# Taking three bits of each weight on ScalarE instead of with a VectorE shift, and a softplus whose sign step reads SBUF

## The chip, the cores and the metric

The kernel runs on one core of a Trainium2 chip. The metric is device time in microseconds. The kernel before takes 617.2 us in the median of 3 runs (616.24 to 618.05).

## What is computed

Inputs are float32 for the attention and float64 for the weights of the two layers. A decaying linear attention (retention) over 2 batches, 8 heads, 768 positions and 64 dimensions gives 1536 tokens of 512 numbers, which then pass two MLP layers of 512 to 2048 to 512. In the reference, cut to what matters:

```python
for t in range(S):
    state = gamma * state + einsum('bhd,bhe->bhde', k[:, :, t], v[:, :, t])
    y[:, :, t] = scale * einsum('bhd,bhde->bhe', q[:, :, t], state)
x = y.transpose(0, 2, 1, 3).reshape(B * S, H * D)

h = x @ w_in                                             # first layer
g = maximum(h, 0) + log1p(exp(-abs(h)))
x = (g @ w_out).astype(float32)

h = x @ w2_in                                            # second layer
x = (h * clip(h + 3, 0, 6) / 6 @ w2_out).astype(float32)
```

## The kernel before

**Products.** Every large product is made of 3 fp32r matmuls: each operand is held as a hi part and a lo part, and hi by hi, hi by lo and lo by hi are summed in PSUM. The names tell the parts: `x_hi` and `x_lo` are the layer's input, `hi` and `lo` the parts of g, `w_parts` holds both parts of a weight chunk.

**Stages.** The attention goes by 12 units of 128 rows. The first four stand in program order. From there on (`nc.on = False`, L310) a planner chooses the order on each engine, and units 4 to 11 are interleaved with the first 8 steps of the first layer (L148 to L154). A layer has 3 chunks of 512 tokens with 16 steps each. A step (L408) does `gemm1` for one block of 128 of the 2048 hidden numbers, 12 matmuls of 128x512 into a PSUM bank h, then the activation to g, hi and lo (L351 to L366), and `gemm2` for the block of two steps earlier (LAG = 2), 12 more matmuls into four held accumulators. A bank comes from eight, four of which are held by the accumulators while the others rotate (L130).

**Weights.** They are float64 in memory, and the 64 chunks of 128 by 512 (32 a layer) are made into two fp32r parts on the chip. `fetch` (L73) loads 512 KB of raw words on SP's queue into one of three `raw` buffers. `convert` (L83) takes the high word y and the low word of each number. ScalarE scales y as a float in place (L89), VectorE clamps it (L90), shifts it by 3 into w (L91), sets the sign bit (L92), and ors in the low word shifted right by 29 (L93). The first 8 chunks then have a ScalarE copy to the hi part and a GpSimd subtraction for the lo part (L96, L97). The other 56 have a negated ScalarE copy to the lo part, a DMA from GpSimd's queue that adds w to it in place (the accumulate transfer, L100), and the ScalarE copy to the hi part. The buffer w has few copies in its pool, so the first operation that writes w waits for the accumulate transfer of an earlier chunk to land.

**When.** `feed` (L119) is called in the steps of the first layer's first chunk (its own weights), in its third chunk (the second layer's w_in, one a step, L415), and in the second layer's first chunk (w_out, L417). Each engine runs its instructions in order, so one that waits holds those behind it. In the trace nearly all instructions carry L31, the line of the helper that records them; tiles are read by name: `raw<-raw` is L89 on ACT and L90 on DVE, `w<-raw` L91, `w<-raw,w` L92 and L93, `w_parts<-w` L96, L99 and L101 on ACT and the accumulate transfer on POOL, `g<-banks` and `e<-g,banks` are L355 and L356, `e<-e` L357, `g<-g,e` L358, `pt` and `qT,kT` the scores of the attention.

Of the kernel before, what the change touches and what calls it, by code (L numbers as in the profile page):

```python
# [10 lines left out]
F32 = mybir.dt.float32  # L11
F32R = mybir.dt.float32r
U32 = mybir.dt.uint32
AF = mybir.ActivationFunctionType
ALU = mybir.AluOpType
PSUM = bass.MemoryType.PSUM
P = 128
# [23 lines left out]
@with_exitstack  # L41
def kernel(ctx, tc, q, k, v, w1_in, w1_out, w2_in, w2_out, tq, tk, tc_, tg, out):
    nc = InOrder(tc)
    B, H, S, D = q.shape
    NT, DM = out.shape
    DFF = w1_in.shape[1]
    NP = H // 2
    KD = DM // P
    NF = DFF // P
    C = P  # L50
    NCH = S // C
    CH = 512
    chunks1 = [(0, 0, 512), (1, 0, 512), (2, 0, 512)]
    chunks2 = [(0, 0, 512), (1, 0, 512), (2, 0, 512)]
    LAG = 2
    EARLY = 4

    tc.nc.scalar.preload_act_table_set("softplus")

    xpool = ctx.enter_context(tc.tile_pool(name="xpool", bufs=1))  # L60
    x_hi = [xpool.tile([P, KD, CH], F32R, name=f"x_hi{c}") for c in range(NT // CH)]
    x_lo = [xpool.tile([P, KD, CH], F32R, name=f"x_lo{c}") for c in range(NT // CH)]

    win_p = ctx.enter_context(tc.tile_pool(name="win", bufs=NF))
    wout_p = ctx.enter_context(tc.tile_pool(name="wout", bufs=NF))
    psum = ctx.enter_context(tc.tile_pool(name="psum", bufs=1, space=PSUM))
    raw_p = ctx.enter_context(tc.tile_pool(name="raw", bufs=3))
    cv_p = ctx.enter_context(tc.tile_pool(name="cv", bufs=2))

    w_in_t, w_out_t, raws = {}, {}, {}  # L70
    words = {0: (w1_in.bitcast(U32), w1_out.bitcast(U32)), 1: (w2_in.bitcast(U32), w2_out.bitcast(U32))}

    def fetch(m, o, f):  # L73
        raw = raw_p.tile([P, CH, 2], U32, tag="raw", name="raw")
        src = words[m][o]
        if o:
            nc.sync.dma_start(out=raw.rearrange("p n t -> p (n t)"), in_=src[f * P:(f + 1) * P, :])
        else:
            nc.sync.dma_start(out=raw.rearrange("p (k n) t -> p k (n t)", k=KD),
                              in_=src[:, 2 * f * P:2 * (f + 1) * P].rearrange("(k p) f -> p k f", p=P))  # L80
        raws[m, o, f] = raw

    def convert(m, o, f):  # L83

        raw = raws.pop((m, o, f))
        low, y = raw[:, :, 0], raw[:, :, 1]

        w = cv_p.tile([P, CH], U32, tag="w", name="w")
        nc.scalar.activation(y.bitcast(F32), y.bitcast(F32), AF.Copy, scale=2.0 ** -112)  # L89
        nc.vector.tensor_scalar(y.bitcast(F32), y.bitcast(F32), -TOP, TOP, ALU.max, ALU.min)  # L90
        nc.vector.tensor_scalar(w, y, 3, None, ALU.logical_shift_left)  # L91
        nc.vector.scalar_tensor_tensor(w, y, 0x80000000, w, ALU.bitwise_and, ALU.bitwise_or)  # L92
        nc.vector.scalar_tensor_tensor(w, low, 29, w, ALU.logical_shift_right, ALU.bitwise_or)  # L93
        t = (wout_p if o else win_p).tile([P, 2, CH], F32R, tag="w", name="w_parts")
        if done[1] < 2 * EARLY:
            nc.scalar.activation(t[:, 0], w.bitcast(F32), AF.Copy)  # L96
            nc.gpsimd.tensor_tensor(t[:, 1], w.bitcast(F32), t[:, 0].bitcast(F32), ALU.subtract)  # L97
        else:
            nc.scalar.activation(t[:, 1], w.bitcast(F32), AF.Copy, scale=-1.0)  # L99
            nc.gpsimd.dma_start(out=t[:, 1].bitcast(F32), in_=w.bitcast(F32), accum_op=ALU.add)  # L100
            nc.scalar.activation(t[:, 0], w.bitcast(F32), AF.Copy)  # L101
        if o:
            w_out_t[m, f] = t
        else:
            w_in_t[m, f] = t.rearrange("p a (k n) -> p a k n", k=KD)

    NU = B * NCH
    order = [(0, 0, f) for f in range(EARLY)]
    for f in range(NF):
        order += [(0, 1, f)] + [(0, 0, f + EARLY)] * (f + EARLY < NF)  # L110
    order += [(1, 0, f) for f in range(NF)] + [(1, 1, f) for f in range(NF)]
    done = [0, 0]

    def fetch_weights(n):
        while done[0] < min(len(order), n):
            fetch(*order[done[0]])
            done[0] += 1

    def feed(n):  # L119

        n = min(n, len(order))
        while done[1] < n:
            fetch_weights(done[1] + (1 if nc.on else 2))
            convert(*order[done[1]])
            done[1] += 1

    banks = psum.tile([P, 8, CH], F32, name="banks")
    free = list(range(8))

    def bank(hold=False):  # L130

        i = free.pop(0)
        if not hold:
            free.append(i)
            return banks[:, i, :]
        return i, banks[:, i, :]

    def release(i):
        free.append(i)

    def first(f):
        return EARLY + 2 * (f + 1) - max(0, f + 1 + EARLY - NF)

    step, last, n_steps = moe(ctx, tc, nc, out, x_hi, x_lo, w_in_t, w_out_t, chunks1, chunks2, NF, KD, DM, CH, LAG, feed, first, bank, release)
    s = 0
    with ExitStack() as actx:
        unit = attention(actx, tc, nc, q, k, v, tq, tk, tc_, tg, x_hi, x_lo, CH, bank, feed, fetch_weights)
        for u in range(CH // P, NU):  # L148
            begin, end = unit(u)
            begin()  # L150
            step(s, True, False)
            end()
            step(s, False, True)
            s += 1  # L154
    while s < n_steps:
        step(s)
        s += 1
# [175 lines left out]
def moe(ctx, tc, nc, out, x_hi, x_lo, w_in_t, w_out_t, chunks1, chunks2, NF, KD, DM, CH, LAG, feed, first, bank, release):  # L333
# [7 lines left out]
    def gemm1(m, c, ci, f):  # L341
        xi, o, n = c
        w = w_in_t[m, f]
        h = bank()[:, :n]
        i = 0
        for kk in range(KD):
            xh, xl = x_hi[xi][:, kk, o:o + n], x_lo[xi][:, kk, o:o + n]
            for a, bb in ((w[:, 0, kk, :], xh), (w[:, 0, kk, :], xl), (w[:, 1, kk, :], xh)):
                nc.tensor.matmul(h, a, bb, start=(i == 0), stop=(i == 3 * KD - 1))
                i += 1  # L350
        e = wk.tile([P, CH], F32, tag="e", name="e")[:, :n]  # L351
        g = wk.tile([P, CH], F32, tag="g", name="g")[:, :n]
        if m == 0:

            nc.scalar.activation(g, h, AF.Relu)  # L355
            nc.vector.scalar_tensor_tensor(e, g, -2.0, h, ALU.mult, ALU.add)  # L356
            nc.scalar.activation(e, e, AF.Softplus)  # L357
            nc.vector.tensor_tensor(g, g, e, ALU.add)  # L358
        else:
            nc.scalar.activation(e, h, AF.Relu, bias=cw)  # L360
            nc.vector.scalar_tensor_tensor(g, e, 6.0, h, ALU.min, ALU.mult)
        hi = gp.tile([P, CH], F32R, tag="hi", name="hi")[:, :n]
        lo = gp.tile([P, CH], F32R, tag="lo", name="lo")[:, :n]
        nc.scalar.activation(hi, g, AF.Copy)
        nc.vector.tensor_tensor(lo, g, hi.bitcast(F32), ALU.subtract)
        g_t[m, ci, f] = hi, lo  # L366
# [41 lines left out]
    def step(s, one=True, two=True):  # L408
        if one and s < len(steps):
            m, c, ci, f = steps[s]  # L410
            gemm1(m, c, ci, f)
            if m == 0 and ci == 0:
                feed(first(f))
            if m == 0 and ci == n1 - 1:
                feed(2 * NF + f + 1)  # L415
            if m == 1 and ci == 0:
                feed(3 * NF + f + 1)  # L417
        if two and LAG <= s < len(steps):
            gemm2(*steps[s - LAG])
        if two and s == len(steps):  # L420
            gemm2(*steps[s - LAG], *(f for _, _, _, f in steps[s - LAG + 1:]))
# [40 lines left out]
```

## Time and profile before

| What | Before |
|---|---|
| runs | 616.24, 617.2, 618.05 us, median 617.2 |
| profiled execution | span 613.8 us; its own time is not given apart |
| TensorE (PE) busy | 598.1 us, 97% of the span |
| VectorE (DVE) busy | 351.8 us, 57% |
| ScalarE (ACT) busy | 275.9 us, 45% |
| GpSimd (POOL) busy | 103.4 us, 17% |
| DMA | 61.60 MB moved, mean 100 GB/s |

The span runs from the first to the last instruction of one execution, and the time of a run has 3.4 us more in the median. Busy shares are means over stretches that differ. In 40 slices of 15.3 us, DVE is at 9 tenths or more from the fourth slice to the tenth, and at 2 or 3 tenths from the 27th on, while PE is at 9 from the fifth slice on, but for the last.

### The profile page before, as it was taken

What the parts mean: (1) busy time and instruction counts of PE and PEld (TensorE: products, weight loads), DVE (VectorE), ACT (ScalarE), POOL (GpSimd) and SP (SyncE); (2) the same over time, 40 slices, a digit from 0 to 9 for tenths busy, and PEclk for the clock granted to TensorE, in tenths of its full rate; (3) what the DMA queues carried; (4) which work ended last, traced back from release to release, by engine and by line L of the source; (5) the groups of instructions that cost most, each with busy time, mean ns of one, the idle gap of its engine ahead of it and who ended that gap; (6) DMA issues with size and microseconds to landing.
All of it is one profiled execution on the core that took longest, in us unless ns stands there. A gap on an engine that the chain in (4) does not pass through costs nothing.

```text
span 613.8 us, 7743 instructions
## 1 busy us (share of the span) xinstructions
PE 598.1 (97%) x2963; PEld 491.2 (80%) x2963; DVE 351.8 (57%) x583; ACT 275.9 (45%) x473; POOL 103.4 (17%) x110
## 2 busy tenths in 40 slices
PE   7988999999999999999999999999999999999997
PEld 6865778788788888888887878888888888888886
DVE  4589999999773334376667798832322222322223
ACT  3355475678563333465556687722222222222220
POOL 1745664432100000011111122200000000000000
PEclk9998999999999999999999999999999999999999
DMA  9998888799600000045566689600100000100001
GB/s 193 236 229 211 219 197 208 192 217 227 159 32 0 1 0 1 9 111 119 140 180 154 162 208 262 125 7 1 68 1 0 1 1 0 70 1 1 0 1 69
DMA packets 69510, 61.60 MB, mean 100 GB/s; under 512 B 40032, under 2 KB 56672, under 8 KB 69472
## 3 DMA queue, kind: packets, MB, share of 16 engines
q1 hardware_dynamic: 61408, 46.42, 26.6%
q0 software_dynamic: 8064, 14.68, 14.6%
q8 instruction: 23, 0.38, 0.3%
q14 instruction: 15, 0.12, 0.1%
HBM read 43.26 MB, written 3.15 MB: 76 GB/s over the span
## 4 chain that ended last, share of the span: by engine, by line
PE 66%; DVE 13%; issue 7%; DMA 6%; ACT 3%; POOL 2%; SPq 1%; DVEq 0%; POOLq 0%; ACTq 0%
PE banks L31 66%; DVE w L31 6%; DMA raw<-in_moe_w_in_dram 3%; DVE raw L31 2%; POOL w_parts L31 2%; DMA w_parts<-w 2%; DVE g L31 1%; SPq L31 1%; DVE pt L31 1%; DMA q<-in_q_dram 1%; DVE lo L31 1%; ACT e L31 1%; DVE e L31 1%; ACT raw L31 1%; ACT w_parts L31 1%
## 5 line engine op out<-in xcount | busy, mean ns | idle before, releaser
L31 PE MATMUL banks<-x_hi,w_parts 128*128 128x512 f32 x768 | 253.9, 391 | 2.4 <-POOL w_parts L31 1.2
L31 PEld LDWEIGHTS banks<-x_hi,w_parts 128*128 128x128 f32 x768 | 143.8, 188 | 34.4 <-POOL w_parts L31 2.1
L31 PE MATMUL banks<-x_lo,w_parts 128*128 128x512 f32 x384 | 149.6, 390 | 0.0
L31 PE MATMUL banks<-hi,w_parts 128*128 128x512 f32 x384 | 129.4, 397 | 0.9 <-POOL w_parts L31 0.8
L31 PE MATMUL banks<-w_parts,hi 128*128 128x512 f32 (+1 forms) x386 | 118.4, 388 | 0.7 <-DVE g L31 0.7
L31 DVE SCALAR_TENSOR_TENSOR g<-e,banks 128x512 f32<-128x512 f32 x48 | 33.0, 687 | 123.3 <-ACT e L31 123.3
L31 DVE SCALAR_TENSOR_TENSOR w<-raw,w 128x512 uint32<-128x512 uint32 x128 | 94.3, 738 | 1.6
L31 DVE TENSOR_TENSOR lo<-g,hi 128x512 fp32r<-128x512 f32 x96 | 66.3, 690 | 48.9 <-ACT hi L31 48.6
L31 POOL DMA_DIRECT2D w_parts<-w x56 | 49.3, 880 | 251.9 <-DVE e L31 98.7
L31 ACT ACTIVATE hi<-g 128x512 fp32r<-128x512 f32 x96 | 60.5, 630 | 65.0 <-DVE g L31 61.6
L31 ACT ACTIVATE e<-banks,three 128x512 f32<-128x512 f32 x48 | 32.9, 686 | 125.7 <-PE banks L31 125.7
L31 ACT ACTIVATE w_parts<-w 128x512 fp32r<-128x512 f32 x120 | 70.4, 625 | 39.2 <-DVE w L31 39.0
L31 PEld LDWEIGHTS banks<-hi,w_parts 128*128 128x128 f32 x384 | 72.8, 190 | 17.6 <-POOL w_parts L31 1.5
L31 PEld LDWEIGHTS banks<-w_parts,hi 128*128 128x128 f32 x386 | 72.3, 188 | 16.0 <-DVE g L31 1.1
L31 PEld LDWEIGHTS banks<-x_lo,w_parts 128*128 128x128 f32 x384 | 72.1, 188 | 14.9
L31 PE MATMUL banks<-lo,w_parts 128*128 128x512 f32 x192 | 75.6, 394 | 0.4 <-DVE lo L31 0.4
L31 PE MATMUL banks<-w_parts,lo 128*128 128x512 f32 (+1 forms) x193 | 74.9, 388 | 0.0
L31 DVE SCALAR_TENSOR_TENSOR e<-g,banks 128x512 f32<-128x512 f32 x48 | 32.7, 682 | 27.5 <-ACT g L31 27.5
L31 DVE TENSOR_TENSOR g<-g,e 128x512 f32<-128x512 f32 x48 | 34.4, 717 | 23.9 <-ACT e L31 23.5
L31 ACT ACTIVATE raw<-raw 128x512 f32<-128x512 f32 x64 | 42.2, 669 | 12.7 <-DMA raw<-in_moe_w_in_dram 12.7
L31 ACT ACTIVATE g<-banks 128x512 f32<-128x512 f32 x48 | 28.2, 587 | 36.5 <-PE banks L31 36.5
L31 PEld LDWEIGHTS banks<-lo,w_parts 128*128 128x128 f32 x192 | 36.5, 190 | 8.9 <-DVE lo L31 1.5
(45 smaller groups left out, 401.1 us busy)
## 6 DMA issues: line engine op xcount, KB each, us to landing
raw<-in_moe_w_in_dram SPq DMA_DIRECT2D x32, 512.0 KB, 4.2
raw<-in_moe_w_out_dram SPq DMA_DIRECT2D x32, 512.0 KB, 4.6
w_parts<-w POOLq DMA_DIRECT2D x56, 256.0 KB, 4.9
q<-in_q_dram SPq DMA_DIRECT2D x12, 256.0 KB, 5.3
v<-in_v_dram SPq DMA_DIRECT2D x12, 256.0 KB, 4.9
k<-in_k_dram SPq DMA_DIRECT2D x11, 256.0 KB, 5.3
out_dram<-ob SPq DMA_DIRECT2D x11, 256.0 KB, 2.0
k<-in_k_dram SPq DMA_DIRECT2D x2, 128.0 KB, 2.8
```

The lines of the kernel that those rows point to most:

```text
L31: ins = getattr(self.engine, op)(*args, **kwargs)
```

## The change

Both parts leave the results of the layer what they were.

The conversion no longer shifts y on VectorE into w. A new ScalarE operation reads the low word as an integer, scales it by a little under 2 to the -29, adds a constant a little under -0.5 from a tile `half` of one number per partition, takes Relu, and writes w as an unsigned integer from 0 to 7. The first VectorE merge sets the sign bit on it as before, and the second now shifts y by 3 and ors w to it. So VectorE has three operations a chunk instead of four, ScalarE has one more, and the first to write w is on ScalarE.

In the softplus, ScalarE copies h instead of taking Relu of it. VectorE sets the sign bit of the copy in SBUF, which gives -|h| (before: -2 Relu(h) + h, which read h in PSUM). The last VectorE step is max(g, 0) + e with two sources, as before g + e. Nothing but the ScalarE copy reads the PSUM bank.

```diff
+    half = raw_p.tile([P, 1], F32, tag="half", name="half", bufs=1)
+    nc.vector.memset(half, -0.5 + 7.5 * 2.0 ** -12)
...
         nc.scalar.activation(y.bitcast(F32), y.bitcast(F32), AF.Copy, scale=2.0 ** -112)
+        nc.scalar.activation(w, low, AF.Relu, scale=2.0 ** -29 * (1 - 2.0 ** -12), bias=half)
         nc.vector.tensor_scalar(y.bitcast(F32), y.bitcast(F32), -TOP, TOP, ALU.max, ALU.min)
-        nc.vector.tensor_scalar(w, y, 3, None, ALU.logical_shift_left)
         nc.vector.scalar_tensor_tensor(w, y, 0x80000000, w, ALU.bitwise_and, ALU.bitwise_or)
-        nc.vector.scalar_tensor_tensor(w, low, 29, w, ALU.logical_shift_right, ALU.bitwise_or)
+        nc.vector.scalar_tensor_tensor(w, y, 3, w, ALU.logical_shift_left, ALU.bitwise_or)
...
-            nc.scalar.activation(g, h, AF.Relu)
-            nc.vector.scalar_tensor_tensor(e, g, -2.0, h, ALU.mult, ALU.add)
+            nc.scalar.activation(g, h, AF.Copy)
+            nc.vector.tensor_scalar(e.bitcast(U32), g.bitcast(U32), 0x80000000, None, ALU.bitwise_or)
             nc.scalar.activation(e, e, AF.Softplus)
-            nc.vector.tensor_tensor(g, g, e, ALU.add)
+            nc.vector.scalar_tensor_tensor(g, g, 0.0, e, ALU.max, ALU.add)
```

The planner then orders the engines anew. Three places show what moves.

ScalarE at the first steps of the first layer's third chunk, where the second layer's weights begin to be converted (`w_parts` are the two copies of a chunk, DMASW stands for the accumulate transfer). Before:

```order
L31 ACTIVATE raw<-raw 128x512 [waits DMAHW6_49]
L31 ACTIVATE g<-banks 128x512 [waits PE_49,Activation_49]
L31 ACTIVATE w_parts<-w 128x512 x2
L31 ACTIVATE e<-e 128x512 [waits DVE_49]
L31 ACTIVATE hi<-g 128x512 [waits DVE_49,PE_49]
L31 ACTIVATE g<-banks 128x512 [waits PE_49,Activation_49]
L31 ACTIVATE w_parts<-w 128x512 [waits DVE_49]
L31 ACTIVATE w_parts<-w 128x512
L31 ACTIVATE e<-e 128x512 [waits DVE_49]
L31 ACTIVATE raw<-raw 128x512 [waits DMAHW7_49]
```

Now:

```order
L31 ACTIVATE raw<-raw 128x512 [waits DMAHW6_49]
L31 ACTIVATE g<-banks 128x512 [waits PE_49]
L31 ACTIVATE w_parts<-w 128x512 x2
L31 ACTIVATE e<-e 128x512 [waits DVE_49]
L31 ACTIVATE hi<-g 128x512 [waits DVE_49,PE_49]
L31 ACTIVATE w<-raw,half 128x512 [waits DMASW2_49,Activation_49]
L31 ACTIVATE g<-banks 128x512 [waits PE_49]
L31 ACTIVATE w_parts<-w 128x512 x2
L31 ACTIVATE e<-e 128x512 [waits DVE_49]
L31 ACTIVATE raw<-raw 128x512 [waits DMAHW7_49]
L31 ACTIVATE hi<-g 128x512 [waits DVE_49,PE_49]
L31 ACTIVATE w<-raw,half 128x512 [waits DMASW3_49,Activation_49]
```

The new operation stands ahead of the scaling of `raw` and of the copy of h, and it carries a wait for an accumulate transfer, which in the rows before no ScalarE instruction has.

VectorE at the same place, before:

```order
L31 TENSOR_SCALAR w<-raw 128x512 [waits DMASW3_49]
L31 SCALAR_TENSOR_TENSOR w<-raw,w 128x512 [waits DVE_49]
L31 TENSOR_SCALAR raw<-raw 128x512 [waits DMAHW0_49,Activation_49]
L31 SCALAR_TENSOR_TENSOR w<-raw,w 128x512 [waits DVE_49]
L31 SCALAR_TENSOR_TENSOR e<-g,banks 128x512 [waits Activation_49]
L31 TENSOR_TENSOR g<-g,e 128x512 [waits Activation_49]
L31 TENSOR_TENSOR lo<-g,hi 128x512 [waits Activation_49]
L31 TENSOR_SCALAR w<-raw 128x512 [waits DMASW4_49]
```

Now:

```order
L31 SCALAR_TENSOR_TENSOR w<-raw,w 128x512 [waits DMASW3_49,Activation_49]
L31 TENSOR_SCALAR raw<-raw 128x512 [waits DMAHW0_49,Activation_49]
L31 SCALAR_TENSOR_TENSOR w<-raw,w 128x512 [waits DVE_49]
L31 TENSOR_SCALAR e<-g 128x512 [waits Activation_49]
L31 SCALAR_TENSOR_TENSOR g<-g,e 128x512 [waits Activation_49]
L31 TENSOR_TENSOR lo<-g,hi 128x512 [waits Activation_49]
L31 SCALAR_TENSOR_TENSOR w<-raw,w 128x512 [waits DMASW4_49,Activation_49]
```

The shift with its wait for the transfer is gone, and the first merge waits for ScalarE too.

TensorE in an attention unit beside the first chunk (`qT,kT` are the scores). Before:

```order
L31 MATMUL banks<-hi,w_parts 128x512
L31 MATMUL banks<-qT,kT 128x128 [waits DVE_49]
L31 MATMUL banks<-qT,kT 128x128 x3
L31 MATMUL banks<-hi,w_parts 128x512
L31 MATMUL banks<-lo,w_parts 128x512
L31 MATMUL banks<-qT,kT 128x128 [waits DVE_49]
L31 MATMUL banks<-qT,kT 128x128 x3
L31 MATMUL banks<-qT,bd_113 128x128 x4
```

Now:

```order
L31 MATMUL banks<-x_lo_62,w_parts 128x512
L31 MATMUL banks<-x_hi_59,w_parts 128x512 x2
L31 MATMUL banks<-qT,kT 128x128 [waits DVE_49,Activation_49]
L31 MATMUL banks<-qT,kT 128x128 [waits DVE_49]
L31 MATMUL banks<-qT,kT 128x128 x6
L31 MATMUL banks<-x_lo_62,w_parts 128x512
L31 MATMUL banks<-x_hi_59,w_parts 128x512 x2
```

The scores of this unit stood in two pieces with fp32r matmuls between, and stand in one.

## Rows read from the trace of the kernel before

**Rows 1.** the page's busy line and its chain by engine

```profile
PE 598.1 (97%) x2963; PEld 491.2 (80%) x2963; DVE 351.8 (57%) x583; ACT 275.9 (45%) x473; POOL 103.4 (17%) x110
...
PE 66%; DVE 13%; issue 7%; DMA 6%; ACT 3%; POOL 2%; SPq 1%; DVEq 0%; POOLq 0%; ACTq 0%
```

**Rows 2.** busy time by stretch: PE, PEld, DVE, ACT, POOL, granted clock, DMA share, GB/s

```profile
30.00:60.00 30.00, 24.83 (x166) 18.39 (x166) 28.18 (x42) 15.97 (x29) 15.73 (x12) 0.94 0.88 223
60.00:120.00 60.00, 57.55 (x387) 46.21 (x384) 57.54 (x96) 35.69 (x66) 33.16 (x30) 0.97 0.81 200
120.00:160.00 40.00, 40.00 (x182) 33.00 (x178) 36.84 (x68) 32.20 (x59) 12.79 (x14) 1.00 0.93 214
350.00:400.00 50.00, 49.31 (x218) 40.37 (x217) 44.79 (x83) 37.61 (x67) 13.10 (x16) 1.00 0.83 197
55.00:65.00 10.00, 9.17 (x35) 6.19 (x34) 10.00 (x17) 4.82 (x9) 5.75 (x4) 0.66 0.70 180
```

**Rows 3.** the chain of waits in order of time, 29 to 48 us: start, us, what

```profile
29.98 0.43 DVE w L31
...
35.72 1.16 DVE w L31
...
47.27 0.68 DVE e L31
47.95 0.34 DVE w L31
```

**Rows 4.** groups by line and form: busy us, mean ns | idle before

```profile
L31 DVE TENSOR_SCALAR w<-raw 128x512 uint32<-128x512 uint32 x64 | 30.6, 480 | 10.2 <-DMA w_parts<-w 9.3 <-DVE raw L31 0.5
```

**Rows 5.** PE's timeline: start, us, operation, [idle before <-releaser]

```profile
78.48 1.16 PE L31 MATMUL banks<-qT,kT 64*128 64x128 f32 x8
...
88.85 0.50 PE L31 MATMUL banks<-x_hi,w_parts 128*128 128x512 f32 x1 [0.40 <-ACT kT L31]
...
102.09 1.26 PE L31 MATMUL banks<-qT,kT 64*128 64x128 f32 x16 [0.63 <-ACT qT L31]
...
110.92 0.66 PE L31 MATMUL banks<-ident,q 128*128 128x128 f32 x4 [1.40 <-DVE e L31]
...
358.13 0.73 PE L31 MATMUL banks<-w_parts,hi 128*128 128x512 f32 x2 [0.69 <-DVE g L31]
```

**Rows 6.** ACT's timeline, 257 to 319 us

```profile
257.19 0.60 ACT L31 ACTIVATE g<-banks 128x512 f32<-128x512 f32 x1 [2.06 <-PE banks L31]
...
262.63 0.60 ACT L31 ACTIVATE g<-banks 128x512 f32<-128x512 f32 x1 [1.89 <-PE banks L31]
...
268.18 0.68 ACT L31 ACTIVATE raw<-raw 128x512 f32<-128x512 f32 x1 [0.57 <-DMA raw<-in_moe_w_in_dram]
268.76 0.58 ACT L31 ACTIVATE g<-banks 128x512 f32<-128x512 f32 x1
269.24 1.14 ACT L31 ACTIVATE w_parts<-w 128x512 fp32r<-128x512 f32 x2
...
294.79 0.59 ACT L31 ACTIVATE g<-banks 128x512 f32<-128x512 f32 x1
...
312.24 0.58 ACT L31 ACTIVATE g<-banks 128x512 f32<-128x512 f32 x1
...
318.60 0.57 ACT L31 ACTIVATE g<-banks 128x512 f32<-128x512 f32 x1
```

**Rows 7.** DVE's timeline, 260 to 288 us

```profile
260.78 0.69 DVE L31 TENSOR_TENSOR lo<-g,hi 128x512 fp32r<-128x512 f32 x1 [0.70 <-ACT hi L31]
...
274.56 0.43 DVE L31 TENSOR_SCALAR w<-raw 128x512 uint32<-128x512 uint32 x1 [1.98 <-DMA w_parts<-w]
...
287.97 0.43 DVE L31 TENSOR_SCALAR w<-raw 128x512 uint32<-128x512 uint32 x1 [2.01 <-DMA w_parts<-w]
```

**Rows 8.** POOL's timeline: the issues of two accumulate transfers

```profile
270.26 0.88 POOL L31 DMA_DIRECT2D w_parts<-w  x1 [5.25 <-ACT w_parts L31]
...
282.86 0.86 POOL L31 DMA_DIRECT2D w_parts<-w  x1 [6.95 <-DVE w L31]
```

## The prediction

> **What bounds the kernel now.** I read the page first: its line of busy time has TensorE (PE) at 97% of the 613.8 us span, VectorE (DVE) at 57% and ScalarE (ACT) at 45%, and its chain of waits is two thirds PE, 13% DVE [rows 1]. Those are averages, so the busy time by stretch comes next [rows 2]. There are two kinds of stretch. From 30 to 120 us, where attention units run beside the first MLP chunk, DVE is busy 85.7 of 90 us while PE has 82.4 of 90: DVE is as full as PE. From 120 us on PE is practically full, and nothing gains by more than the few stalls left. ACT is full nowhere, but has 32.2 of 40 us at 120 to 160 and 37.6 of 50 at 350 to 400, the two other stretches in which weights are converted. One row stands out: at 55 to 65 us the granted clock is 0.66, most of it at the lower level of 1.2 GHz instead of 2.4, after a stretch in which PE had waited again and again. Then the chain in order of time: between 28 and 56 us it runs almost wholly through DVE, and the shift that the change removes is a piece of it [rows 3]. Last, PE's own timeline gives the idle time it had, and who ended it [rows 5]. What can be won is this: the DVE chain at 28 to 56 us, PE's idle pieces of 60 to 120 us, a stall at 358 us.
>
> **The edits.** A conversion loses a DVE shift, 480 ns in the mean [rows 4] (64 conversions), and gains an ACT operation of the same size with a bias per partition. That form stands nowhere on a strided integer source; ACT's copy of the other half of the same buffer is the nearest row, 0.68 us long and 0.58 us from start to start [rows 6]; a floor is a copy from PSUM, 0.48 from start to start [rows 6]. I take 0.66 us alone and 0.57 in a row. Softplus has the same count of operations; its first DVE step no longer reads PSUM, and the bank of h is free after ACT's copy instead of after that DVE step (0.68 us at 47.27 [rows 3]). The memset runs once at the start; the load of constants there hides it, and if not it costs below 0.1 us.
>
> **A, 28 to 56 us.** Four shifts stand on the chain by themselves, the first with 0.43 us, then 1.16, 0.43 again, and the last 0.34 [rows 3], 2.4 us. A fifth lies in a merged piece and I put it at 0.34 like its neighbour: 2.7. The new first step of softplus on the chain (0.68 at 47.27 us [rows 3]) goes from SBUF to SBUF like the shift, 0.43 where undisturbed, so 0.25 less. Sum -3.0. If ACT or the weights' transfers are late next, it is 0; if DVE's neighbours shorten as well, -5. I take -3.0, as ACT had 16 of 30 us there [rows 2], and some ten new operations add 6.6.
>
> One thing in rows 3 speaks for caution: the same shift took 0.43 us once and 1.16 us another time, with a GpSimd (POOL) operation beside it. The step that read PSUM was never stretched. So the new step can be. The Trainium skill, SBUF — State Buffer, section *Who interferes with whom*, states that a one-source VectorE operation from SBUF to SBUF can take the port pair shared with GpSimd, whichever starts first holding it. By that the 0.25 falls away and A would be -2.7; the trace agrees as to the shift.
>
> **B, 56 to 122 us.** PE waited 0.40 us for ACT kT, 0.63 for ACT qT and 1.40 for a DVE e that held a PSUM bank [rows 5]: 2.4 us. The last goes since the copy on ACT releases the bank; the two others hang on ACT copies, which waited for room in DVE's queue further up, and go as DVE falls behind less. DVE loses 20 shifts here, some 12 us of 86. Also the score matmuls of three units stood in two pieces of four, one head group each, with other matmuls between; now one unit's do, and its pieces stand next to each other. In the trace such a piece of 8 records takes 1.16 us (78.48, and again 81.61), a whole unit of 16 records 1.26 (102.09) [rows 5]: 2.32 - 1.26 = 1.06 more for a unit in two pieces. Two units fewer could give 2.1 at most, or nothing where PE then waits for something else; I take half, 1.0. Sum of B -3.4, bounds 0 and -4.5. The half-clock stretch I leave as it is.
>
> **C, 120 to 170 us.** Some 13 conversions fall in the stretch of 40 us. At 0.57 each they bring ACT's 32.2 us [rows 2] to 39.6 of 40. So ACT is full, though it isn't late by much: +0.5, bounds 0 and +3.
>
> **D, 256 to 323 us: the change moves a wait.** A conversion's buffer w is free when the accumulate transfer that reads it has landed. Its first writer was the DVE shift: it waited there 1.98 and 2.01 us [rows 7], and ACT went on with the next g. Now the first writer is the ACT operation, and behind it in ACT's queue stand raw, the PSUM copy g, and the negated copy that issues the next transfer. For six chunks the wait is for a copy that stands just one step before, so a ring closes: from the negated copy's start to the POOL issue 1.02 us (269.24 to 270.26, [rows 6, 8]), to landing 4.30 and 5.11 us (270.26 to 274.56 and 282.86 to 287.97, [rows 7, 8]), where I take 4.7; then the new operation 0.66, raw 0.58 and g 0.48 (268.18, 268.76, 269.24 [rows 6]). That is 7.44 us a turn, where PE brings a new h each 5.44 (257.19 to 262.63 [rows 6]); in two of the six turns no raw copy stands, 6.86. Together 4 x 2.0 + 2 x 1.42 = 10.8 us of lag. Now g gets to 7.0 us of lag: ten steps after 257.19 it would be due at 311.6, and it starts at 318.60 [rows 6]; its four turns from 294.79 on are paced by the raw buffers at 5.82 us ((312.24 - 294.79) / 3 [rows 6]); they come after the six here too and add 4 x 0.38 = 1.5: 12.3 in all. Part of a lag is hidden: g of a step is multiplied two steps later, 10.9 us after it is due, and from g's start to the end of lo it takes 4.28 (257.19 to 261.47 [rows 6, 7]), which leaves some 6.3 after the first matmul. Of a lag of 12.3, 6 becomes PE stall. By the same working 7.0 - 6.3 = 0.7 is stall now, and with PE's slow start after it I count 1.2. So **+4.8**. With every landing at 4.30 the six turns lose 8.4 and the cost is +2.4, with every landing at 5.11 13.3 and +7.3; the landings mix, so I keep +2.4 and +7.3 as ends only.
>
> **E, 350 to 360 us.** PE stalls 0.69 us for DVE g at 358.13 [rows 5], 0.4 more with weight loads. DVE is there busy 44.8 of 50 us, and loses 16 shifts. -1.0, bounds 0 and -1.1. ACT gets 16 operations, 37.6 + 9.1 = 46.7 of 50 [rows 2]. What covers this is the lag allowed between gemm1 and gemm2; without it 1 to 3 us would show.
>
> **Sum**: -3.0 - 3.4 + 0.5 + 4.8 - 1.0 = -2.1 us. It is made against the profiled span of 613.8; its own time isn't listed, and the median of the runs, 617.2, stands 3.4 us over it, which I leave as it is: **615.1 us**. That is 0.34% faster, just past 0.3% (1.85 us), which is about what a measurement of this kernel can tell from no change.
>
> **Rivals.** *The clock fall goes too.* PE's short waits before 55 us are shorter with A, so the stretch at 0.66 may not come: 10 x (1 - 0.66) = 3.4 us at most [rows 2], some 3.1 as part of it overlaps with waits. Time 615.1 - 3.1 = 612.0. Against it: the first eight weight chunks still go through POOL at the same place. Chance 0.17.
>
> *ACT becomes the bound from 28 us on, and it is slower.* ACT is in order, and the new operation stands ahead of copies that PE or DVE wait for (g, kT, hi). It decides as soon as it starts later than the DVE shift did. Then A and B shrink to -0.5 each and C goes to +2: -0.5 - 0.5 + 2 + 4.8 - 1.0 = +4.8, time 622.0; with half of that 619.5. For it: ACT at 39.6 of 40 us. Against it: 36 of 60 us at 60 to 120 [rows 2]. The Trainium skill, ScalarE: Activation LUTs, *Rules for kernel authors*, advises VectorE rather than ScalarE for relu and add; here the rows bear it out in price, 0.68 against 0.43. Chance 0.25.
>
> *The wait of D costs nothing.* It decides if landing takes under 2.7 us (5.44 - 1.02 - 0.66 - 0.58 - 0.48). 615.1 - 4.8 = 610.3 us. Both rows say over 4, so the chance is only 0.10, most of it for slack I don't see.
>
> *D takes place, A isn't won in full*, as transfers (DMA share 0.88 and 0.81 [rows 2]) feed DVE next: A and B -1.5 each, so 617.2 - 3.0 + 0.5 + 4.8 - 1.0 = 618.5. Chance 0.13.
>
> **Numbers.** The forecast keeps 0.35, with a range of its own from 612.5 to 618. Faster by over 0.3% (below 615.35): just over half the forecast (0.19), the clock and the costless wait, 0.19 + 0.17 + 0.10 = 0.46. Slower (above 619.05): ACT as bound, nearly all of it, and a third of the last, 0.26. The same: 0.28. The range runs from 610 to 621.5, leaving out some of the fastest and of the slowest case.
>
> **What would show it.** A: in the chain from 28 to 56 us DVE pieces are shorter, and PE's first full stretch begins some 3 us sooner. B: no PE wait for DVE e. C: ACT over 95% busy at 120 to 160. D: ACT waits for the accumulate transfer, six turns of over 7 us between copies g from 256 us on, and PE idle for DVE lo or ACT hi of about 5 us before 325 us. E: no stall near 358 us. I am wrong if turns stay near 5.44, if PE waits for ACT before 120 us, or if the clock stays at 1.00 throughout.

## The result and the profile after

The changed kernel takes 622.63 us in the median of 10 runs (621.39 to 624.0), the kernel before 618.33 of 10 (615.55 to 622.21): a ratio of 1.0076, with a 95% interval from 1.0051 to 1.0101. It is slower, by some 4 to 5 us.

The profiled execution of the change has a span of 621.9 us and a time of 623.69: 1.8 us lie outside the span, and the spans of its nine other runs stand as far below their times. By that the execution profiled before, with 613.8 us, took some 615.6, which is at the lower end of its runs. So the two profiles differ by 8.1 us where the medians differ by 4.3.

The page's busy line and chain of the change, to hold against [rows 1]:

```profile
PE 599.3 (96%) x2963; PEld 489.5 (79%) x2963; DVE 320.2 (51%) x520; ACT 314.9 (51%) x537; POOL 105.2 (17%) x110
...
PE 62%; DMA 8%; issue 7%; ACT 4%; DVE 2%; POOL 1%; DVEq 0%; ACTq 0%; POOLq 0%; SPq 0%
```

VectorE lost 31.6 us of work and ScalarE gained 39.0. DVE's part in the chain fell from 13% to 2%, while transfers went from 6% to 8% and ACT from 3% to 4%. But the chain of the change is followed back only to 99.3 us, so its shares add up to 84% and say nothing on the stretch from 28 to 56 us. Behind 99 us VectorE's w operations alone had 4.7% of the chain before and have 0.5% now, so there VectorE did leave it. The busy time by stretch (columns as in [rows 2]):

```profile
30.00:60.00 30.00, 25.14 (x165) 18.49 (x166) 28.03 (x40) 20.10 (x36) 18.72 (x13) 0.95 0.94 246
60.00:120.00 60.00, 56.48 (x405) 46.58 (x402) 55.97 (x88) 49.80 (x88) 34.54 (x32) 1.00 0.88 212
120.00:160.00 40.00, 40.00 (x178) 33.14 (x177) 29.97 (x54) 35.66 (x65) 10.25 (x12) 1.00 0.81 198
250.00:326.00 76.00, 72.69 (x302) 56.78 (x300) 38.39 (x67) 45.52 (x81) 9.56 (x11) 0.98 0.49 116
...
350.00:420.00 70.00, 66.34 (x284) 52.34 (x283) 42.55 (x72) 49.41 (x87) 13.04 (x15) 1.00 0.60 139
55.00:65.00 10.00, 8.90 (x48) 6.31 (x49) 9.93 (x12) 7.31 (x13) 4.93 (x5) 0.83 0.65 183
290.00:295.00 5.00, 5.00 (x17) 3.71 (x15) 2.66 (x5) 4.04 (x8) 0.86 (x1) 0.73 0.18 31
```

and two stretches of the kernel before that the prediction had not listed:

```profile
250.00:326.00 76.00, 75.67 (x333) 62.01 (x332) 49.32 (x85) 42.81 (x76) 10.40 (x12) 1.00 0.51 122
350.00:420.00 70.00, 69.31 (x306) 56.94 (x305) 50.41 (x91) 42.89 (x75) 13.10 (x16) 1.00 0.59 141
```

The number of matmuls in a stretch (behind the x) tells the loss. TensorE did 302 of them from 250 to 326 us where it had done 333, and 284 from 350 to 420 us where it had done 306; one takes 0.225 us when nothing waits (222 in 50 us), so that is 7.0 and 5.0 us. Some records may be missing, so times of the same work tell it better. Two marks are good for that: ScalarE's 33rd copy g, the first of the third chunk (row 257.19 in [rows 6]), and VectorE's scaling of the first output tile. From the second mark to the end of the span it takes 173.6 to 173.9 us in the kernels compared.

| Kernel | to the 33rd g | from there to the first output | span |
|---|---|---|---|
| before | 257.19 | 182.86 | 613.8 |
| before, a second profile | 256.86 | 182.36 | 612.9 |
| the change | 252.83 | 195.16 | 621.9 |

The change **wins 4.4 us before the first mark and loses 12.3 us between the two**. ScalarE's timeline behind the first mark shows how (g are the copies that TensorE's work comes from, w the new operation):

```profile
252.83 0.60 ACT L31 ACTIVATE g<-banks 128x512 f32<-128x512 f32 x1 [2.33 <-PE banks L31]
...
257.71 0.76 ACT L31 ACTIVATE w<-raw,half 128x512 uint32<-128x512 uint32 x1 [1.27 <-DMA w_parts<-w]
258.37 0.58 ACT L31 ACTIVATE g<-banks 128x512 f32<-128x512 f32 x1
...
265.62 0.76 ACT L31 ACTIVATE w<-raw,half 128x512 uint32<-128x512 uint32 x1 [2.23 <-DMA w_parts<-w]
...
266.83 0.59 ACT L31 ACTIVATE g<-banks 128x512 f32<-128x512 f32 x1
...
274.42 0.75 ACT L31 ACTIVATE w<-raw,half 128x512 uint32<-128x512 uint32 x1 [4.00 <-DMA w_parts<-w]
275.08 0.58 ACT L31 ACTIVATE g<-banks 128x512 f32<-128x512 f32 x1
...
282.36 0.75 ACT L31 ACTIVATE w<-raw,half 128x512 uint32<-128x512 uint32 x1 [3.28 <-DMA w_parts<-w]
...
283.58 0.59 ACT L31 ACTIVATE g<-banks 128x512 f32<-128x512 f32 x1
...
290.13 0.76 ACT L31 ACTIVATE w<-raw,half 128x512 uint32<-128x512 uint32 x1 [2.91 <-DMA w_parts<-w]
...
291.36 0.59 ACT L31 ACTIVATE g<-banks 128x512 f32<-128x512 f32 x1
```

The wait that stood on DVE before (1.98 and 2.01 us in [rows 7]) is now on ACT, with 1.27 to 4.00 us, and the next g stands behind it. From 258.37 to 291.36 four turns (a turn is the time from one g to the next) take 8.25 us each in the mean, where TensorE needs 5.44. (Before, single turns were as long, 7.85 us from 273.51 to 281.36, but each was followed by a shorter one.) The same wait comes again from 350 us on, at the second layer's w_out:

```profile
346.13 1.14 ACT L31 ACTIVATE w_parts<-w 128x512 fp32r<-128x512 f32 x2
...
352.07 0.75 ACT L31 ACTIVATE w<-raw,half 128x512 uint32<-128x512 uint32 x1 [1.43 <-DMA w_parts<-w]
...
378.70 0.75 ACT L31 ACTIVATE w<-raw,half 128x512 uint32<-128x512 uint32 x1 [2.78 <-DMA w_parts<-w]
...
386.92 0.75 ACT L31 ACTIVATE w<-raw,half 128x512 uint32<-128x512 uint32 x1 [2.50 <-DMA w_parts<-w]
```

TensorE's timeline shows where it hurts, and two places before 120 us that have changed hands:

```profile
87.55 1.16 PE L31 MATMUL banks<-qT,kT 64*128 64x128 f32 x14 [1.31 <-DVE bd L31]
...
99.81 1.16 PE L31 MATMUL banks<-qT,kT 64*128 64x128 f32 x14 [1.11 <-DVE bd L31]
...
287.27 0.50 PE L31 MATMUL banks<-hi,w_parts 128*128 128x512 f32 x1 [1.89 <-ACT hi L31]
...
362.56 0.73 PE L31 MATMUL banks<-w_parts,hi 128*128 128x512 f32 x2 [1.59 <-DVE x_lo L31]
...
388.76 0.73 PE L31 MATMUL banks<-w_parts,hi 128*128 128x512 f32 x2 [0.72 <-ACT hi L31]
```

Of [rows 5], the waits for kT, qT and the bank held by e are gone, and two for DVE bd stand there, 2.42 us together; the stall at 358.13 came back larger. And the chain of waits, in order of time, is the ring itself: transfer, new operation, raw, g, negated copy, transfer. Its last row here is the transfer that the operation at 352.07 us waits for.

```profile
259.88 5.66 DMA w_parts<-w
...
265.62 0.76 ACT w L31
266.38 0.56 ACT raw L31
266.94 0.48 ACT g L31
267.42 0.53 ACT w_parts L31
...
268.34 6.00 DMA w_parts<-w
...
347.15 4.83 DMA w_parts<-w
```

### The profile page after: what moved, and what is told of

Same layout as the page of the kernel before. It is cut to its first block, busy times and chain, and to the rows that moved or that the text cites. A ratio compares the mean times of both kernels' runs of the same rounds, so it can differ in the third digit from the quotient of the medians.

```text
span 621.9 us, 7785 instructions
## 1 busy us (share of the span) xinstructions
PE 599.3 (96%) x2963; PEld 489.5 (79%) x2963; DVE 320.2 (51%) x520; ACT 314.9 (51%) x537; POOL 105.2 (17%) x110
## 4 chain that ended last, share of the span: by engine, by line
PE 62%; DMA 8%; issue 7%; ACT 4%; DVE 2%; POOL 1%; DVEq 0%; ACTq 0%; POOLq 0%; SPq 0%
PE banks L31 62%; DMA w_parts<-w 4%; DMA raw<-in_moe_w_in_dram 3%; ACT w_parts L31 1%; POOL w_parts L31 1%; ACT raw L31 1%; ACT w L31 1%; DVE w L31 0%; ACT g L31 0%; ACT e L31 0%; DVE raw L31 0%; DVE g L31 0%; DVE lo L31 0%; ACT hi L31 0%; DVE bd L31 0%
## 5 line engine op out<-in xcount | busy, mean ns | idle before, releaser
L31 DVE TENSOR_TENSOR lo<-g,hi 128x512 fp32r<-128x512 f32 x96 | 68.2, 711 | 55.9 <-ACT hi L31 54.4
L31 ACT ACTIVATE w<-raw,half 128x512 uint32<-128x512 uint32 x64 | 48.4, 758 | 29.2 <-DMA w_parts<-w 29.2
L31 DVE SCALAR_TENSOR_TENSOR g<-g,e 128x512 f32<-128x512 f32 x48 | 34.0, 708 | 25.3 <-ACT e L31 24.9
```

The costliest lines, as they stand in the source:

```text
L31: ins = getattr(self.engine, op)(*args, **kwargs)
```

## The experiments

Two theories stood against each other. **Theory 1**: the wait for the accumulate transfer, which the change moved from VectorE's queue into ScalarE's, costs the time. **Theory 2**: ScalarE's added load costs it (64 operations of 0.76 us, 48.4 us in all), wherever it waits. Ratios are to the kernel before on the same chip, with 95% intervals.

**1. The wait put back, the load kept.**

```diff
-        nc.scalar.activation(w, low, AF.Relu, scale=2.0 ** -29 * (1 - 2.0 ** -12), bias=half)
+        nc.scalar.activation(low, low, AF.Relu, scale=2.0 ** -29 * (1 - 2.0 ** -12), bias=half)
...
-        nc.vector.scalar_tensor_tensor(w, y, 0x80000000, w, ALU.bitwise_and, ALU.bitwise_or)
+        nc.vector.scalar_tensor_tensor(w, y, 0x80000000, low, ALU.bitwise_and, ALU.bitwise_or)
```

> The whole change, but ScalarE writes the three bits back into the raw buffer in place of the low word, and VectorE's first merge is the first to write w. ScalarE has the same number of operations and the same busy time (about 315 us); only the wait for the accumulate transfer is back on VectorE. Theory 1 (the wait that moved into ScalarE's queue costs the time): turns between copies g from 250 us on are at most 6 us again, the losses of some 7 us before 326 us and some 5 us after 350 us go, the gain of some 4.4 us before 250 us stays; 613 to 616 us. Theory 2 (ScalarE's added load costs it, wherever it waits): 621 us or more, as with the change.

Measured: 616.48 us, ratio 0.9975 (0.9951 to 1.0000), 6.2 us below the change. Between the marks it takes 182.42 us, as before:

```profile
60.00:120.00 60.00, 53.76 (x366) 43.70 (x366) 53.13 (x82) 46.22 (x83) 32.08 (x31) 0.94 0.86 207
250.00:326.00 76.00, 75.59 (x331) 61.47 (x330) 41.16 (x72) 47.27 (x84) 9.57 (x11) 1.00 0.48 117
350.00:420.00 70.00, 70.00 (x310) 57.77 (x309) 42.91 (x74) 48.68 (x86) 13.03 (x15) 1.00 0.60 139
```

The 331 and 310 matmuls of the last two rows are back, with ACT about as busy as in the change. "At most 6 us" for a turn was wrong: single turns of 10.28 and 8.14 us stand there, with ScalarE waiting 3.90 us for DVE e, but each is followed by one under 6, and TensorE does not stall for them. So it is long turns in a row that cost, not a long turn. And the planner ordered the first 120 us anew, and there the gain is lost: 260.61 us to the first mark, 366 matmuls where the change had 405, at a granted clock of 0.94. That part of the expectation was wrong too, and where that order loses its time stays open.

**2. The wait alone.** The kernel before, with

```diff
         nc.scalar.activation(y.bitcast(F32), y.bitcast(F32), AF.Copy, scale=2.0 ** -112)
+        nc.scalar.activation(w[:, :1], low[:, :1], AF.Copy)
```

> The kernel before with one more ScalarE operation in each conversion, which writes a single column of w, so that the first write of w and its wait for the accumulate transfer are on ScalarE; the shift on VectorE then overwrites the column, and VectorE's work is as before. The operation adds some 0.2 us each. Theory 1 (moved wait): turns of over 7 us from 250 us on as in the change, no gain before 250 us; 624 to 631 us. Theory 2 (load): 64 operations of 0.2 us are 13 us of ScalarE beside 276, nowhere near full; within 2 us of the kernel before.

Measured: 626.11 us, ratio 1.0119 (1.0077 to 1.0161). An operation of 0.20 us, 13 us of ScalarE in all, costs 8.3 us in the median. Two of its waits:

```profile
277.53 0.20 ACT L31 ACTIVATE w<-raw 128x1 uint32<-128x1 uint32 x1 [1.91 <-DMA w_parts<-w]
...
297.35 0.20 ACT L31 ACTIVATE w<-raw 128x1 uint32<-128x1 uint32 x1 [2.70 <-DMA w_parts<-w]
```

Its turns are 7.94, 5.10, 7.53, 7.20 and 6.84 us, three long ones in a row where before had none, and shorter than the change's as the operation is shorter; it takes 186.33 us between the marks, 3.5 more than before. The rest of the loss lies before the first mark (264.88 us), so this kernel shows the ring without its load, but its total is not the price of the ring: a single small operation also made the planner order the first 120 us otherwise.

**3 and 4. Each half of the change by itself.** The conversion with the old softplus, and the softplus with the old conversion (the two halves of the diff above).

> The conversion of the change, the softplus of before. Theory 1: the losses after 250 us stay whole (12 us against the profiled execution of before), of the gain of 4.4 us before 250 us the shift's part of some 3; 623 to 626 us. A rival for where the gain comes from (the PSUM bank released earlier and the lighter softplus step): no gain before 250 us, 626 us or more.

Measured: 618.87 us, 1.0016 (0.9992 to 1.0040). The ring is there (turns of 8.5, 7.8, 8.5 and 7.9 us after the first), 189.24 us between the marks. The loss from 350 us on is not: TensorE is busy 70.00 of 70 us there, and no ScalarE wait for a transfer stands in that stretch. So the expectation of 623 or more was wrong: the second loss does not follow from the conversion alone, but hangs on the planner's order as well, which is another here.

> The softplus of the change, the conversion of before. Theory 1: no turn over 6 us from 250 us on and no loss there; before 120 us the wait of TensorE for a bank that VectorE held goes; 615 to 618 us. The rival, that the gain comes from the softplus: 614 us or less. If the softplus part itself is what slows the layers: 620 us or more.

Measured: 618.18 us, 1.0016 (0.9988 to 1.0044). Between the marks it takes 180.86 us, 2.0 less than before. Single turns of 7.5 us stand there as in the kernel before; "no turn over 6 us" was written too sharply here, and so were the bounds of experiments 8 (7.56 us) and 10 (9.65 us). By itself the softplus neither wins nor loses.

**5, 6 and 7. More buffers.** In the change, and in the kernel before, w is taken from four or six buffers in turn:

```diff
-        w = cv_p.tile([P, CH], U32, tag="w", name="w")
+        w = cv_p.tile([P, CH], U32, tag=f"w{done[1] % 4}", name="w", bufs=1)
```

> The whole change with four buffers w used in turn, so that ScalarE's first write of w waits for the accumulate transfer of four chunks earlier everywhere; in the change it is two chunks at the start of the second layer's weights and three after it. Work, load and the place of the wait are those of the change. Theory 1 (the wait in ScalarE's queue, as far as the transfer it waits for is recent): a transfer of four steps earlier has landed, so no turn of over 6 us from 250 us on, and no loss there; 614 to 618 us. Theory 2 (ScalarE's added load): as the change, 621 us or more.

> As the run before with six buffers w, so that a conversion finds its buffer free for two chunks more. Theory 1: with four the wait is gone already, so this is the same within 0.3%, 614 to 618 us; where it is faster still, waits on four stood in the first 120 us. Theory 2: 621 us or more.

> The kernel before with six buffers w. VectorE waits 9.3 us in all for these transfers there, which its idle time hides for the most part. Theory 1: 616 to 618 us, so that what six buffers give the change comes from ScalarE's queue and not from the buffers as such. Rival: the buffers by themselves give 3 us or more, 615 us or less, and the runs with more buffers say nothing on where the wait stands.

Measured: 653.26 us (1.0575, 1.0535 to 1.0614), 636.10 (1.0301, 1.0263 to 1.0339) and 626.91 (1.0151, 1.0116 to 1.0185). All three expectations fell. The waits of ScalarE's first write of w in the run with four buffers, and in the change (total us, times, longest):

```profile
ACT w L31 <- DMA w_parts<-w: 51.5, 21, 5.7
```

```profile
ACT w L31 <- DMA w_parts<-w: 29.2, 13, 4.0
```

With four buffers the waits are more, not fewer. With six they are fewer (23.2 us in 8), and the kernel is still slower than the change. GpSimd's issues of the accumulate transfer in the run with four show the ring going on beyond 328 us, at 7 to 9 us a turn, and below them stands one of ScalarE's waits:

```profile
264.13 0.86 POOL L31 DMA_DIRECT2D w_parts<-w  x1 [4.67 <-PE banks L31]
272.58 0.88 POOL L31 DMA_DIRECT2D w_parts<-w  x1 [7.59 <-ACT w_parts L31]
280.69 0.87 POOL L31 DMA_DIRECT2D w_parts<-w  x1 [7.24 <-ACT w_parts L31]
```

```profile
269.86 0.75 ACT L31 ACTIVATE w<-raw,half 128x512 uint32<-128x512 uint32 x1 [2.21 <-DMA w_parts<-w]
```

The operation at 269.86 us waits for the transfer issued at 264.13, one step earlier, although its buffer is one of four. As I read the order, the conversion runs four chunks ahead there instead of two, and the planner puts the new operation of the fourth chunk at once behind the copy that will free its buffer. By this reading it is the place in the queue, and not the number of buffers, that decides how long the queue is held; no run tests it by itself. What makes six buffers cost the kernel before 9 us was not settled: ScalarE waits 10.3 us there for raw words of w_out, which it had not to wait for before, and the loss lies both before the first mark (264.30) and behind it (188.03).

**8 to 10. The change in one layer, and the load without the wait.** First the new conversion for the first layer alone (the old one for the second layer; the new softplus throughout):

```diff
-        nc.scalar.activation(w, low, AF.Relu, scale=2.0 ** -29 * (1 - 2.0 ** -12), bias=half)
+        if m == 0:
+            nc.scalar.activation(w, low, AF.Relu, scale=2.0 ** -29 * (1 - 2.0 ** -12), bias=half)
```

and so for the merges, with the old three VectorE operations in the other case.

> The new conversion for the first layer's 32 chunks alone, the old one for the second layer's; the new softplus throughout. Theory 1: the gain before 250 us stays, and the waits of the second layer's chunks are back on VectorE: 613 to 617 us, no turn of over 6.2 us after 250 us. If the loss after 250 us stays, it comes from what the first layer leaves behind (lag or buffers) and not from these chunks' own wait: 621 us or more.

Measured: **609.86 us**, 0.9878 (0.9844 to 0.9912), 252.58 us to the first mark and 181.28 between the two; the 613 to 617 us expected were too high. Then with the second layer's w_in too (`if m == 0 or o == 0`):

> The new conversion for the first layer's chunks and the second layer's first 16 (w_in), the old one for its last 16 (w_out); the new softplus throughout. The first 250 us have the instructions of the run with the first layer alone (609.86 us). Theory 1: the ring between 250 and 326 us is back, with turns over 7 us and a loss of 5 to 7 us there, and there is no loss from 350 to 420 us: 614 to 618 us. If the two losses hang together (the lag of the first makes the second), both are back: 620 us or more.

Measured: 617.42 us, 1.0003 (0.9978 to 1.0029); 253.99 and 188.71. Then the first layer alone as above, and in the second layer the new operation in place, as in experiment 1:

> The run with the first layer alone, and for the second layer's chunks the ScalarE operation too, but written in place into the raw buffer, so that ScalarE has the load of the whole change (some 315 us) and none of its waits from 250 us on. Theory 1 (the wait, not the load): 608 to 613 us, no turn of over 6.2 us after 250 us. Theory 2 (the load in the second layer's conversions costs it): 615 us or more.

Measured: 614.03 us, 0.9937 (0.9910 to 0.9964); 255.55 and 181.31. The stretches 250 to 326 and 350 to 420 us of the three, in this order:

```profile
250.00:326.00 76.00, 75.88 (x335) 62.47 (x335) 48.28 (x89) 43.98 (x80) 11.37 (x13) 1.00 0.56 132
350.00:420.00 70.00, 70.00 (x310) 57.99 (x309) 45.42 (x81) 39.95 (x70) 11.57 (x14) 1.00 0.52 123
```

```profile
250.00:326.00 76.00, 72.03 (x306) 57.83 (x304) 38.55 (x67) 45.18 (x80) 9.57 (x11) 0.98 0.48 112
350.00:420.00 70.00, 70.00 (x310) 57.99 (x309) 49.30 (x89) 42.87 (x76) 13.87 (x16) 1.00 0.60 144
```

```profile
250.00:326.00 76.00, 76.00 (x336) 62.64 (x335) 44.10 (x78) 51.07 (x91) 10.44 (x12) 1.00 0.54 132
350.00:420.00 70.00, 70.00 (x309) 57.69 (x309) 40.91 (x70) 47.49 (x83) 12.15 (x14) 1.00 0.50 116
```

The w_in chunks alone bring back the first loss (306 matmuls for 335) and not the second. With the load but not the wait, ACT is as busy as in the change (51.07 and 47.49 us), and between the marks it takes 181.31 us against 181.28 without the load: in the second layer the load costs nothing. The 4.2 us in the median by which this run is over the one with the first layer alone stand ahead of the first mark, as far as the profiles show them (3.0), where the planner's order differs from that run's; I had taken 613 as the upper end and missed by 1.

**11. The old softplus with the first layer's conversion.**

> The run with the first layer alone, with the softplus of before. It splits the gain of 7.9 us: if the softplus gives part of it (the bank released by ScalarE's copy, the lighter VectorE step), 611 to 615 us; if the shift alone gives it, 609 to 610.5 us; with the softplus alone the kernel was 618.18 us, level with before.

Measured: 611.59 us, 0.9912 (0.9880 to 0.9944); 254.21 and 181.91. So the softplus may give 1.7 of the 7.9 us (the intervals of the two runs overlap, so this is not clear of noise), and nothing in the total where VectorE still has its shift (experiment 4).

**12. The kernel before once more.**

> The kernel before, unchanged, for a second profile: its runs lie between 615 and 622 us, and the first profile is of one of the fastest. If the spread comes from the clock in the stretch beside the attention, the stage from the first conversion of the second layer's weights to the first output tile takes 182.9 us again, within 0.5, and what differs lies before 180 us, with granted clocks below 1.00 there. If the second stage varies by itself by several us, the losses measured there in single profiles say less than they seem to.

Measured: 617.2 us (614.72 to 620.07), a profile of 612.9 us at a granted clock of 1.00 throughout. Its first stretches:

```profile
30.00:60.00 30.00, 24.89 (x176) 18.86 (x176) 28.19 (x42) 16.13 (x29) 15.73 (x12) 1.00 0.92 227
60.00:120.00 60.00, 55.02 (x375) 43.80 (x373) 58.72 (x96) 35.59 (x66) 32.90 (x30) 1.00 0.81 200
```

Between the marks it takes 182.36 us, within 0.5 as expected. The stretch at half clock of [rows 2] isn't there, and yet the first mark comes only 0.33 us sooner (256.86): TensorE did 10 matmuls more up to 60 us, 12 fewer from 60 to 120 us (375 instead of 387), and waited, at 65.07 and again at 66.76 us (0.71):

```profile
65.07 0.50 PE L31 MATMUL banks<-hi,w_parts 128*128 128x512 f32 x1 [1.84 <-ACT w_parts L31]
```

What the clock took in the first profile was hidden there behind the engines that fed TensorE. That does not hold for the spread of the runs (615 to 622 us), which goes with the mean granted clock: of its 80 executions in these experiments, the 15 at 1.00 took 615.4 us in the median, the 34 at 0.992 to 0.994 617.9, the 11 at 0.990 and below 621.5. Where the clock fell in those is not profiled.

## Why the prediction was wrong

It forecast 615.1 us, between 610.0 and 621.5; the measured 622.63 lies above both.

**The base.** I took 3.4 us outside the span, from the median of three runs; it is 1.8, and the rest of the 3.4 was that the profiled execution lay under the median. A sum against the profile would have started from 615.6; with that it would have been 613.5, further off. The ten runs of the kernel before have a median of 618.33, 1.1 over the three that I had; the other 6.4 of the 7.5 us missed are the change, +4.3 measured for -2.1 forecast.

**The edits.** The new operation takes 0.76 us, 0.65 from start to start, against my 0.66 and 0.57; the softplus step in SBUF 0.45 against 0.68 in PSUM:

```profile
L31 ACT ACTIVATE w<-raw,half 128x512 uint32<-128x512 uint32 x64 | 48.4, 758 | 29.2 <-DMA w_parts<-w 29.2
...
L31 DVE TENSOR_SCALAR e<-g 128x512 uint32<-128x512 uint32 x48 | 21.6, 451 | 31.7 <-ACT g L31 31.6
```

**A, B and C: the sum nearly right, the pieces not.** -5.9 was forecast to the first mark, -4.4 came. ScalarE's copies g tell where. The third starts at 51.19 us where it was 54.22, A's 3.0 us; but the fourth comes no sooner (66.73 for 66.47), as TensorE waits 2.28 us at 55.78 for GpSimd's part of w_parts, where it had waited 0.83, and other orders changed too. So A ended at 0, much as in the condition that I had named for it, with the weights late next. From there to the eighth g (115.28 for 120.89) the change won 5.6 us, more than B's 3.4. (B's 20 shifts, 12 of 86 us, are those of 30 to 120 us and so take in A's; from 56 us on it is some 14.) The waits named in B went, and two for DVE bd, 2.4 us, came in their place. DVE stayed busy 84.0 of 90 us between 30 and 120: it did about two conversions more, and some of what was left grew slower. Beside GpSimd's operations two of seven lo took 1.53 and 1.77 us (956 ns in the mean of all seven, before 679), and the new step e took 585 ns there against 451 in the whole span. That last is the case for which the Trainium skill, SBUF — State Buffer, section *Who interferes with whom*, says that a one-source step from SBUF can meet GpSimd; the trace agrees: 0.69 and 1.49 us in the two that ran beside GpSimd's work on w_parts, 0.41 or 0.42 in the other six. C did not come: ACT was busy 35.66 of 40 us from 120 to 160, not 39.6, and PE 40.00 of 40 as before. Of the 5.6 us, 1.2 were lost again by the first mark, and no run says to what.

The clock's fall at 55 to 65 us shrank to 0.83. In the one pair of profiles that can be compared (experiment 12) such a fall was worth 0.33 us and not the 3.1 of the rival; over all executions time does go with the clock.

**D: the mechanism right, the size too small.** The ring, its turn of over 7 us and its stall for ACT hi and DVE lo came as described. The first turn was 5.54, the next four 8.46, 8.25, 8.50 and 7.78, where I had 7.44 and 6.86: landings took up to 6.0 us (268.34 in the chain) where I had 4.7, and the operation 0.76. Five turns instead of six, 11.3 us of lag instead of 10.8. What it costs is told by experiments 8 and 9: 188.71 - 181.28 = 7.4 us between the marks, and 7.6 us in the medians, against +4.8. My own upper end, +7.3, was the measured value. TensorE's waits for ACT hi and DVE lo before 325 us come to 2.8 us, not to about 5. Part of the rest is the clock: after the stall of 1.89 us at 287.27 the granted clock is 0.73 from 290 to 295 us, 1.4 us of work, which I had not priced.

**E: the step that failed.** I wrote "-1.0, bounds 0 and -1.1", and that the lag allowed between gemm1 and gemm2 covers ScalarE's 16 operations there; a wait for the transfer stood in E at nothing. In the change the same wait as in D came at w_out, with 1.43 to 2.78 us, and cost 195.16 - 188.71 = 6.5 us between the marks (against experiment 9; 5.2 in the medians, as the change is 1.2 quicker to the first mark). I had weighed ScalarE's load in that stretch (46.7 of 50 us), which by experiment 10 costs nothing, and not asked again, chunk by chunk, which transfer the operation waits for. For the chunks at 256 us I had taken a copy one step before as the reason; in the second layer it is no other: the transfer that the operation at 352.07 us waits for began at 347.15, behind a copy of 346.13. The gain forecast in E was not the shifts' either: the stall at 358 us is gone in experiments 4 and 8 too, where VectorE keeps its shift in the second layer. Between the marks experiment 4 takes 2.0 us less than before, experiment 8 1.6 (182.86 - 181.28).

Together: -4.4 to the first mark, then -1.6 + 7.4 + 6.5 = 12.3, which is 7.9 of the 8.1 us between the profiles. Between the marks the forecast had 4.8 - 1.0 = 3.8. Of the 8.5 us missed there, 7.5 are E's and 2.6 D's, less the 1.6.

**The rivals.** "ACT becomes the bound from 28 us on" gave 622.0 us, near the measured time, by luck: the first 250 us got faster, and in the second layer ACT's load is not what costs (experiment 10). (With half of it the sum is 619.6, not 619.5.) Its condition, an operation that starts later than the shift did, is the right one, in the wrong place. "The wait of D costs nothing" needed landings under 2.7 us; none came near.

What is shown: the wait's place costs the time (experiments 1, 8, 9 and 10), the load does not, in the second layer. The second loss needs the planner's order too: experiment 3 has the new conversion and no such wait behind 350 us. Argued only: that the planner's position of the new operation, and not the number of buffers, sets which transfer it waits for; the run with four buffers agrees with it, but it changed other orders too.

## What to carry to other kernels

When an operation moves to another engine, ask first which waits move with it, and what stands behind it in the new queue: here a wait of 2 us that VectorE could afford held ScalarE's copies, and through them the transfer it was waiting for, so that it closed a ring. Then ask that for every stretch in which the operation stands, not only where the chain shows it. The same operation can be had without the wait (written into a buffer that is already there) or only where the engine it relieves is the bound: the conversion of the first layer alone is 1.2% faster than before, where the whole change is 0.8% slower.

## What the runs showed that I had not expected

More buffers did not help: with four ScalarE waited 51.5 us in 21 waits, in the change 29.2 us in 13, and the kernel went from 622.6 to 653.3 us; with six it waited 23.2 us in 8, and the kernel still took 636.1.

A stretch at the lower clock can cost next to nothing: two profiles of the kernel before, one with a granted clock of 0.66 from 55 to 65 us and one at 1.00, reach the first mark within 0.33 us of each other. But its executions at a mean clock of 0.990 and below took 6.0 us more in the median than those at 1.00, so a fall is not free wherever it stands.

One ScalarE operation of 0.20 us per conversion, or another number of buffers, moves the planner's order of the first 120 us enough to shift the first mark by 7 us (264.88 and 264.30 against 257.19; some of it is the clock, 0.94 from 60 to 120 us in both against 0.97), so a total time alone does not price such an edit.
